# Retention attention and routed experts on one core: the passage from attention to the first expert is rearranged (digits of nine chunks at once, search tables in halves on VectorE, rows in half blocks, two weight chunks ahead of the gather)

## Chip, cores and metric

The kernel runs on one core of a Trainium2 chip. The metric is device time in microseconds (us) of one execution, taken as the median of several runs. Engines: PE is TensorE (matrix products), DVE is VectorE, ACT is ScalarE, POOL is GpSimd, SP is the engine that here issues the plain DMAs.

## What is computed

The reference, cut to what matters: a causal retention attention, and a mixture of experts with one expert per token, whose tokens are handed out greedily in the order of their logits and with a fixed capacity of 576 for each of the eight experts.

```python
# attention: B=8, H=8, S=576, D=64
scores = scale * np.matmul(q, k.transpose(0, 1, 3, 2))
ret = scores * Dmat[None]            # gamma[h] ** (i - j) for i >= j, else 0
x = np.matmul(ret, v)                # then laid out as 4608 tokens x 512
# experts: N=4608 tokens, D=512, E=8, F=1024, cap=576
logits = x @ w_gate
for idx in np.argsort(-logits.flatten()):
    tok, e = idx // E, idx % E
    if assigned[tok] >= 0 or counts[e] >= cap: continue
    assigned[tok] = e; counts[e] += 1
for e in range(E):
    mask = assigned == e
    out[mask] = np.maximum(x[mask] @ w1[e], 0.0) @ w2[e]
```

## The kernel before

**Attention** (lines 484 to 847) works through 16 units, four batch pairs of four head pairs each; a unit has nine blocks of 128 positions. For every batch pair it leaves the transposed tokens in the tile `xT` (four head pairs of 128 rows by 1152 tokens). Out of these come the logits (`logits`, `logits2`), in 36 chunks of 128 tokens, nine per batch pair, and the tokens as rows in a DRAM buffer `xd`: by VectorE (`rows`) for the first three pairs, by PE (`rows_pe`, one block of 128 tokens, four head pairs, a ScalarE copy L711 and a write to `xd` on SP's queue L712) for the last. The table `fill`, written through `at(g, ...)`, says after which block a piece of this side work stands in the program.

**Routing** is done expert by expert: the kernel finds which expert fills first, at which logit, and lists its tokens. The first such search (`search_first`, L250) looks for the bound digit by digit, in five digits of 7, 7, 6, 6 and 6 bits. It needs, for every chunk, the digits of the best logit (`first_digits`, tiles `DF` and `D2`) and a table of comparisons for each digit from the second on (`first_table`, tiles `FT`). In the kernel before, digits of the last nine chunks are made three chunks at a time, interleaved with the counting of the first digit (`count_first`, `count_first_pe`); of the 128-wide table of these chunks, eight are made one by one by GpSimd (`first_table_slow`), the rest by VectorE during the search (`s.pending`). A round of the search is: PE sums flags (L259), VectorE takes the digit `j` (L261), marks the chunks' candidates `oe` (L269), updates the running value `vl`, `vf` (L275, L277), PE counts with the tables (L291, and L292 for what was carried), VectorE compares (L295 to L302). Where PE would idle, `s.idle` puts in a piece of the remaining `rows_pe` blocks, or matmuls on a constant tile (`warm`).

After the search come `members` and `listing` (the index tile `idx` of the first expert, L463), then `leave` (L483), which takes the expert's tokens out of the logits.

**Experts.** For each expert the rows of its 576 tokens are gathered in five pieces by GpSimd's indirect DMA (`gather`, L946, tile `xg`; four pieces of 128 tokens, one of 64), turned over by PE (`transposes`, L962) and split by ScalarE and VectorE into a rounded part `xh` and a rest `xl` (L964, L965). The weights come in eight chunks of 512 KB per expert (`dma_pump`, L916, SP's queue, tile `raw`, four buffers; chunks 0 to 3 are w1, 4 to 7 are w2). `conv` splits a chunk: ScalarE writes the rounded part (`w1h`, `w2h`, L930) and the negated copy (`w1l`, L934), and a GpSimd DMA adds `raw` to it (L935); with `fast` VectorE subtracts instead (L932). `l1` does 16 blocks of 12 matmuls (`ph`, L991: four contraction slices by three products of the parts; blocks alternate between 256 and 320 tokens, for expert 0 blocks 0 and 1 have 256, 2 and 3 have 320), each followed by ScalarE and VectorE (`hb`, L995, L998); two blocks in f use one w1 chunk with two token halves, so blocks 0 to 3 need chunk 0, 4 to 7 chunk 1, 8 to 11 chunk 2. `l2` (L1030, `py`) does the second product.

What orders the work: engines run their own queues in program order. `Mixer` interleaves the routing of the next expert (`phases`) with the matmuls by estimated times. `state['most']` caps how many weight chunks `dma_pump` may issue, so it decides at which place of SP's queue a load stands. In the kernel before, four chunks are issued as soon as the first expert is known, one is converted (`fast`) before its tokens arrive, and three more after blocks 0, 1 and 2 of `l1`.

```python
state = dict(dma=0, conv=0, most=4, listing=-1)          # before, L876
        gather(0)                                         # L1068
        conv(True)
        mix.step()
        warm(20)
```

Of the kernel before, what the change touches and what calls it, by code (L numbers as in the profile page):

```python
# [82 lines left out]
class Route:  # L83
# [14 lines left out]
    def setup(s):  # L98
# [17 lines left out]
        s.DF, s.inc, s.sm, s.oz, s.D1 = T("DF", [5, 36], BF16), T("inc", [5], I32), T("sm", [2, 5], I32), T("oe", [43, 8], BF16), T("D1", [36], F32)  # L116
# [53 lines left out]
    def first_digits(s, c0, c1):  # L170
# [8 lines left out]
        if c1 > 24:  # L179
            V.tensor_copy(s.D1[:, c0:c1], d[:, 1])  # L180
# [6 lines left out]
    def first_table(s, i, g0, g1):  # L187
        n, k = g1 - g0, widths(FIRST)[i]
        if k == 64:
            n *= 4  # L190
            s.nc.vector.tensor_tensor(s.FT[i][:, 4*g0:4*g1].rearrange("p c (k w) -> p c k w", w=2),
                                      s.k64[:, None, :].rearrange("p o (k w) -> p o k w", w=2).to_broadcast([128, n, 32, 2]),
                                      s.D2[:, i-2, 4*g0:4*g1, None, :].to_broadcast([128, n, 32, 2]), op=ALU.is_le)
            return
# [55 lines left out]
    def search_first(s):  # L250
# [5 lines left out]
        yield 300, 30  # L256
        for i, K in enumerate(KK):
# [15 lines left out]
            oh = s.oe  # L273
            t = pool.tile([128, 36], F32, name="vl")
# [3 lines left out]
            if i == 0 and len(s.pending) > 3:  # L278
                s.pending.pop(0)()
# [7 lines left out]
            for n, (a, b) in enumerate(pieces):  # L287
                yield 200, 25*(b - a)
                for c in range(a, b, w):
                    st = s.FT[i+1][:, c:c+2].rearrange("p c k -> p (c k)") if w == 2 else s.FT[i+1][:, c//4, :, c % 4]  # L290
                    nc.tensor.matmul(cw, st, s.oz[:, c+w-1:c+w+7].rearrange("p c e -> p (c e)"), start=(c == 0), stop=False, skip_group_check=True)  # L291
            nc.tensor.matmul(cw[:, 64-8*w:72-8*w], sel.to_broadcast([128, 128]), cp, start=False, stop=True, skip_group_check=True)  # L292
# [4 lines left out]
            else:  # L297
# [4 lines left out]
                V.tensor_tensor(cp[:64], own[0], x, op=ALU.add)  # L302
            s.idle("row")
# [76 lines left out]
    def members(s, p):  # L380
# [24 lines left out]
        if not p:  # L405
            s.idle("rows")
            s.idle(2)
# [9 lines left out]
    def listing(s, p):  # L417
# [25 lines left out]
        if not p:  # L443
            s.idle("rows")
            s.idle(6)
# [63 lines left out]
def attention(tc, nc, P, qk, vk, cst_d, wg_d, rf, xd, Lg):  # L509
# [187 lines left out]
    def rows_pe(bp, blk, product=False, hps=range(HP)):  # L697
# [4 lines left out]
        for hp in hps:  # L702
            o, x = pt[:, hp*128:(hp+1)*128], XT[bp][:, hp, blk*128:(blk+1)*128]
            if product:
                nc.tensor.matmul(o, x, ident, start=True, stop=True)
            else:
                nc.tensor.transpose(o, x, ident)
# [31 lines left out]
    for bp in range(NP):  # L739
        g0 = (bp+1)*4*NB + 2  # L740
        for k, b0 in enumerate((0, 3, 6)):
# [11 lines left out]
            else:  # L753
# [3 lines left out]
                else:  # L757
                    at(G-1, lambda it: rest(both(it, R.first_digits(27, 30))), it)
# [3 lines left out]
    for bp in range(3):  # L762
        g0, it = (bp+1)*4*NB + 2, R.first_digits(9*bp, 9*bp+9)
        for i in range(10):
            at(g0+22+i//3, next, it, None)
        for n, (i, a, b) in enumerate(((1, 0, 1), (1, 1, 2), (2, 0, 2), (3, 0, 2), (4, 0, 2))):
            at(g0+24+2*n, R.first_table, i, 2*bp+a, 2*bp+b)
# [59 lines left out]
    left = [lambda b=b: rows_pe(bp, b, b > 0) for b in range(NB)]  # L827
# [8 lines left out]
    R.first_table_slow(1, 24, 28)  # L836
    b = R.first_digits(30, 33)
# [42 lines left out]
def moe(tc, nc, P, R, xd, w1_d, w2_d, out, mix):  # L880
# [5 lines left out]
    state = dict(dma=0, conv=0, most=4, listing=-1)  # L886
    RAW, W1, W2, XH, XL = {}, {}, {}, {}, {}
    scat = []
    spacer = P['c'].tile([1, 1], F32, name="spacer")
# [79 lines left out]
    def l1(e, tr):  # L969
# [5 lines left out]
        for i, (f, s) in enumerate(order):  # L975
# [25 lines left out]
            if s and f in (1, 2, 4, 6) or e == 0 and i < 3:  # L1001
# [62 lines left out]
    def run():  # L1064
# [4 lines left out]
        conv(True)  # L1069
        mix.step()  # L1070
        warm(20)
# [3 lines left out]
        warm(3)  # L1075
# [74 lines left out]
```

## Time and profile before

| | us |
|---|---|
| median of 3 runs | 664.94 (661.15 to 668.07) |
| the profiled execution's own time | 667.28 |
| its span, first to last instruction | 665.5 |
| PE busy in the span | 633.5 (95%) |
| DVE busy | 420.1 (63%) |
| ACT busy | 273.1 (41%) |
| POOL busy | 180.7 (27%) |

The profile is of one execution. Times in rows are us from the span's start. A row of a timeline is a start, a duration, the engine, the line in the kernel, the operation, the tiles (written <- read), and the number of instructions merged; in square brackets stands how long the engine idled before it and what ended that. A row of the chain of waits is a start, a duration, and what the work that ended last was doing or waiting for then. PEclk is the share of TensorE's full clock that was granted.

### The profile page before, as it was taken

What the parts mean: (1) busy time and instruction counts of PE and PEld (TensorE: products, weight loads), DVE (VectorE), ACT (ScalarE), POOL (GpSimd) and SP (SyncE); (2) the same over time, 40 slices, a digit from 0 to 9 for tenths busy, and PEclk for the clock granted to TensorE, in tenths of its full rate; (3) what the DMA queues carried; (4) which work ended last, traced back from release to release, by engine and by line L of the source; (5) the groups of instructions that cost most, each with busy time, mean ns of one, the idle gap of its engine ahead of it and who ended that gap; (6) DMA issues with size and microseconds to landing.
All of it is one profiled execution on the core that took longest, in us unless ns stands there. A gap on an engine that the chain in (4) does not pass through costs nothing.

```text
span 665.5 us, 14105 instructions
## 1 busy us (share of the span) xinstructions
PE 633.5 (95%) x5381; PEld 542.3 (81%) x5383; DVE 420.1 (63%) x1603; ACT 273.1 (41%) x488; POOL 180.7 (27%) x233
## 2 busy tenths in 40 slices
PE   8999999999879998999999999998999999999995
PEld 6887877886659876987897798788879989978984
DVE  3577878788856987887897799587775302311200
ACT  2333333333227343554356156334724733652601
POOL 2221222122122116125143141332224134131111
PEclk8999999999988999999999999999999999999998
DMA  9995999974367749879499659928884995894521
GB/s 335 402 366 158 302 313 293 282 245 102 133 225 157 161 143 224 220 204 244 140 217 232 193 144 211 247 86 186 203 224 112 202 271 152 181 257 133 96 63 39
DMA packets 51699, 134.71 MB, mean 202 GB/s; under 512 B 5808, under 2 KB 19760, under 8 KB 51632
## 3 DMA queue, kind: packets, MB, share of 16 engines
q1 hardware_dynamic: 36528, 81.65, 36.5%
q0 software_dynamic: 14960, 51.91, 35.7%
q8 instruction: 42, 0.69, 0.4%
q10 hardware_dynamic: 144, 0.26, 0.1%
q14 instruction: 25, 0.20, 0.1%
HBM read 81.90 MB, written 18.87 MB: 151 GB/s over the span
## 4 chain that ended last, share of the span: by engine, by line
PE 66%; DVE 13%; issue 10%; DMA 6%; ACT 2%; POOL 2%; SPq 0%; POOLq 0%; DVEq 0%; ACTq 0%
PE py L1030 24%; PE ph L991 20%; PE pA L584 4%; PE pX L636 4%; PE pX L626 3%; PE pS L601 3%; DMA qin<-in_qk 2%; PE pt L962 2%; DMA raw<-in_w 2%; PE r L341 2%; PE pT L665 1%; DVE G L168 1%; PE pX L624 1%; DMA cst<-in_cst 1%; DMA w2l<-raw 1%
## 5 line engine op out<-in xcount | busy, mean ns | idle before, releaser
L1030 PE MATMUL py<-w2h,hb 128*128 128x512 f32 x576 | 188.3, 399 | 0.0
L991 PE MATMUL ph<-xh,w1h 128*128 128x320 f32 (+1 forms) x512 | 153.7, 305 | 1.4 <-ACT xh L964 0.7
L991 PE MATMUL ph<-xl,w1h 128*128 128x320 f32 (+1 forms) x512 | 150.5, 298 | 1.0 <-issue 1.0
L991 PE MATMUL ph<-xh,w1l 128*128 128x320 f32 (+1 forms) x512 | 150.4, 298 | 0.0
L1030 PE MATMUL py<-w2l,hb 128*128 128x512 f32 (+1 forms) x320 | 125.5, 392 | 0.1
L1030 PEld LDWEIGHTS py<-w2h,hb 128*128 128x128 f32 x576 | 104.0, 188 | 20.7
L991 PEld LDWEIGHTS ph<-xh,w1h 128*128 128x128 f32 x512 | 97.6, 193 | 3.7 <-ACT xh L964 1.6
L991 PEld LDWEIGHTS ph<-xl,w1h 128*128 128x128 f32 x512 | 97.3, 192 | 1.8 <-issue 1.2
L998 DVE SCALAR_TENSOR_TENSOR hb<-ph,hb 128x256 fp32r<-128x256 f32 (+1 forms) x192 | 58.8, 351 | 61.9 <-ACT hb L995 57.0
L991 PEld LDWEIGHTS ph<-xh,w1l 128*128 128x128 f32 x512 | 97.4, 192 | 0.0
L995 ACT ACTIVATE hb<-ph 128x256 fp32r<-128x256 f32 (+1 forms) x128 | 51.4, 409 | 106.6 <-PE ph L991 98.5
L607 ACT ACTIVATE S<-pS,cst 64x128 f32<-64x128 f32 x128 | 46.4, 363 | 96.6 <-PE pS L601 94.9
L1007 POOL DMA_INDIRECT out_y<-yt,idx x40 | 40.9, 1022 | 118.2 <-ACT yt L1047 75.4
L1030 PEld LDWEIGHTS py<-w2l,hb 128*128 128x128 f32 (+1 forms) x320 | 56.7, 177 | 14.0 <-DMA w2l<-raw 1.5
L564 POOL TENSOR_TENSOR ks<-nin,cst 128x512 f32<-128x512 f32 x32 | 33.3, 1058 | 113.7 <-DMA nin<-in_vk 102.4
L1047 ACT ACTIVATE yt<-py 128x512 f32<-128x512 f32 x32 | 19.1, 598 | 105.3 <-PE py L1030 79.7
L935 POOL DMA_DIRECT2D w2l<-raw x32 | 28.9, 902 | 122.5 <-ACT hb L995 118.7
L589 DVE TENSOR_TENSOR am<-pA,cst 128x512 f32<-128x512 f32 x64 | 41.1, 683 | 22.1 <-PE pA L584 15.6
L946 POOL DMA_INDIRECT xg<-xd,idx x40 | 40.4, 1010 | 51.7 <-issue 27.0
L1050 DVE TENSOR_TENSOR yt<-yt,py 64x512 f32<-64x512 f32 x8 | 5.4, 679 | 69.9 <-ACT yt L1049 69.8
L935 POOL DMA_DIRECT2D w1l<-raw x31 | 27.7, 907 | 59.4 <-ACT w1l L934 36.8
L584 PE MATMUL pA<-qin,kin 64*128 64x128 f32 x512 | 38.3, 289 | 1.6 <-DMA qin<-in_qk 1.6
(190 smaller groups left out, 968.7 us busy)
## 6 DMA issues: line engine op xcount, KB each, us to landing
raw<-in_w SPq DMA_DIRECT2D x64, 512.0 KB, 6.5
w2l<-raw POOLq DMA_DIRECT2D x32, 512.0 KB
w1l<-raw POOLq DMA_DIRECT2D x31, 512.0 KB
kin<-in_qk SPq DMA_DIRECT2D x14, 576.0 KB
qin<-in_qk SPq DMA_DIRECT2D x14, 576.0 KB
vin<-in_vk SPq DMA_DIRECT2D x14, 576.0 KB, 11.0
nin<-in_vk SPq DMA_DIRECT2D x14, 512.0 KB, 7.7
xd<-xr SPq DMA_DIRECT2D x36, 192.0 KB, 4.2
```

The costliest lines, as they stand in the source:

```text
L564: nc.gpsimd.tensor_tensor(KS[u][:, a:b], LD[u, 'n'].rearrange("p (a d) -> p a d", d=64)[:, a:b], ks[:, u % HP, a:b, None].to_broadcast([12 ...
L584: nc.tensor.matmul(PA[0][h][:, j], LD[u, 'k'][r, s], LD[u, 'q'][r, s], start=True, stop=True, skip_group_check=True)
L589: nc.vector.tensor_tensor(am, PA[0][h], m[:, None, h, :].to_broadcast([128, n, 128]), op=ALU.mult)
L607: nc.scalar.activation(st[64*h:64*h+64, :, 64*h:64*h+64], PS[u][64*h:64*h+64], AF.Copy, scale=ss[64*h:64*h+64, hp, c:c+1])
L636: nc.tensor.matmul(px[64*h:64*h+64, :], v[:, blk*128+64*h:blk*128+64*h+64], AM[g, h], start=False, stop=blk < 8, skip_group_check=True)
L935: nc.gpsimd.dma_start(lo, raw, accum_op=ALU.add)
L946: nc.gpsimd.indirect_dma_start(out=xg[:n, j, :], out_offset=None, in_=xd[:, :], in_offset=bass.IndirectOffsetOnAxis(ap=found[e][:n, j:j+1] ...
L991: T.matmul(ps, w, x, start=(k == 0), stop=(k == 11))
L995: A.activation(hb[:, f, c], ps, AF.Relu)
L998: V.scalar_tensor_tensor(hb[:, f, to+a:to+b], ps[:, a:b], 0.0, hb[:, f, 256*s+a:256*s+b].bitcast(F32), op0=ALU.max, op1=ALU.subtract)
L1007: st = nc.gpsimd.indirect_dma_start(out=out[:, :], out_offset=bass.IndirectOffsetOnAxis(ap=found[e][:n, t:t+1], axis=0), in_=y[:n], in_off ...
L1030: T.matmul(ps[:m], a, w, start=(k == 0), stop=(k == last), skip_group_check=True)
```

## The change

- **Digits**: `first_digits` for chunks 27 to 35 is one call of nine chunks instead of three of three; its first two instructions stand ahead of the last count, and the copy `D1` is gone.
- **Tables**: `first_table_slow` is gone. VectorE makes the 128-wide table of the last twelve chunks in one instruction in the search's first round, and the three 64-wide tables in halves of six chunks. One table of the third batch pair stands earlier in attention.
- **Search**: the product for what was carried (L292) stands between the two pieces of the counting matmuls. Idle places of PE are filled otherwise: rows are plain transposes in half blocks, `"rows"` is one such half and two constant matmuls, and `members` and `listing` have constant matmuls only.
- **Weights**: two chunks are issued before the gather, both are converted fast. A 1-element DMA on SP's queue reads the third gathered piece, and the next loads stand behind it. The other six chunks of expert 0 are converted after blocks 3, 5, 7, 9, 11 and 13. There are 25 and 4 constant matmuls around the first transposes in place of 20 and 3.

```diff
@@ first_digits, first_table
-        if c1 > 24:
-            V.tensor_copy(s.D1[:, c0:c1], d[:, 1])
...
-    def first_table_slow(s, i, c0, c1):
-
-        for c in range(c0, c1):
-            k = widths(FIRST)[i]
-            s.nc.gpsimd.tensor_scalar(s.FT[i][:, c//4, :, c % 4], s.kt[:, :k, 0], s.D1[:, c:c+1], None, op0=ALU.is_le)
@@ search_first
         yield 300, 30
+        s.idle("row")
...
             oh = s.oe
+            if i == 0:
+                s.pending.pop(0)()
             t = pool.tile([128, 36], F32, name="vl")
...
-            if i == 0 and len(s.pending) > 3:
-                s.pending.pop(0)()
             if s.pending:
                 s.pending.pop(0)()
...
-            nc.tensor.matmul(cw[:, 64-8*w:72-8*w], sel.to_broadcast([128, 128]), cp, start=False, stop=True, skip_group_check=True)
+                if n == 0:
+                    nc.tensor.matmul(cw[:, 64-8*w:72-8*w], sel.to_broadcast([128, 128]), cp, start=False, stop=False, skip_group_check=True)
...
+            if s.pending:
+                s.pending.pop(0)()
             s.idle("row")
@@ attention, its end
-            at(g0+24+2*n, R.first_table, i, 2*bp+a, 2*bp+b)
+            at(g0+24-2*(bp == 2)+2*n, R.first_table, i, 2*bp+a, 2*bp+b)
...
-    some(3)
-    rest(both(R.count_first(33, 36), b))
-    R.first_table_slow(1, 28, 32)
-    c = R.first_digits(33, 36)
+    some(4)
+    rest(R.count_first(33, 36))
+    c = R.first_digits(27, 36)
+    for _ in range(2):
+        next(c)
     R.count_first_pe([27, 30, 33], **tag())
     rest(c)
-    R.pending = [lambda: R.first_table(1, 8, 9)] + [lambda i=i: R.first_table(i, 6, 9) for i in (2, 3, 4)]
-    some(1)
-    return R, [lambda b=b, h=h: rows_pe(bp, b, True, h) for b in range(NB - len(left), NB) for h in [(x,) for x in range(HP)]]
+    R.pending = [lambda: R.first_table(1, 6, 9)] + [lambda i=i, a=a, b=b: R.first_table(i, a, b) for i in (2, 3, 4) for a, b in ((6, 7.5), (7.5, 9))]
+    return R, [lambda b=b, h=h: rows_pe(bp, b, h) for b in range(NB - len(left), NB) for h in (range(2), range(2, HP))]
@@ moe
-    state = dict(dma=0, conv=0, most=4, listing=-1)
+    state = dict(dma=0, conv=0, most=2, listing=-1)
...
-            if s and f in (1, 2, 4, 6) or e == 0 and i < 3:
+            if e == 0 and i == 4:
+                state['most'] = 8*E
+            if i in ((3, 5, 9, 13) if e else (3, 5, 7, 9, 11, 13)):
                 conv()
...
         conv(True)
+        conv(True)
         mix.step()
-        warm(20)
+        warm(25)
...
-        warm(3)
+        warm(4)
...
-        state['most'] = 8*E
+
+        nc.sync.dma_start(spacer2, XG[0][0:1, 2, 0:1])
+        state['most'] = 4
+        dma_pump()
```

On VectorE, at the end of attention and the start of the search, there stand before the digits of the last three chunks alone (`om`, `dg`, `DF`, `D` are what `first_digits` writes, `f` and `cp` come of the first count, `j` is the first digit):

```order
L248 TENSOR_TENSOR cp_2297<-cnt,room_473 128x8
L156 TENSOR_SCALAR om<-m 128x3
L158 TENSOR_TENSOR om<-m,om 128x3
L177 TENSOR_TENSOR dg<-om,sm 128x5x3
L177 TENSOR_TENSOR dg<-dg,sm 128x5x3
L180 CAST D_490<-dg 128x3
L181 TENSOR_TENSOR DF<-dg,inc 128x5x3
L183 TENSOR_TENSOR D_491<-dg,inc 128x3x6
L261 TENSOR_REDUCE j<-r 128x1
```

and now those of all nine, whose two `om` have already run, and behind the marks `oe` the tables `FT`:

```order
L240 TENSOR_TENSOR cp_2282<-cnt,room_473 128x8
L177 TENSOR_TENSOR dg<-om,sm 128x5x9
L177 TENSOR_TENSOR dg<-dg,sm 128x5x9
L179 TENSOR_TENSOR DF<-dg,inc 128x5x9
L181 TENSOR_TENSOR D_490<-dg,inc 128x3x18
L254 TENSOR_REDUCE j<-r 128x1
L262 SCALAR_TENSOR_TENSOR oe<-DF,j,oh 128x112
L265 TENSOR_SCALAR sel<-rc_f,j 128x1
L262 SCALAR_TENSOR_TENSOR oe<-DF,j,oh 128x176
L193 TENSOR_TENSOR FT_497<-kt,DF 128x1536
L270 TENSOR_SCALAR vl<-DF,j 128x36
L272 TENSOR_TENSOR vf<-vl,DF 128x36
```

Three digit instructions fewer stand between `cp` and `j`, and a table of 1536 elements in place of 512 stands between `oe` and `vl`.

On SP's queue, where the first expert `e` is read, there stood before:

```order
L712 DMA xd<-xT 128x512 x8
L896 TENSOR_LOAD e
L896 ISA x2
L712 DMA xd<-xT 128x512
L916 ISA
L916 DMA raw<-in_w 128x1024
```

and now (`spacer` is the 1-element DMA):

```order
L703 DMA xd<-xT 128x512 x9
L885 TENSOR_LOAD e
L885 ISA x2
L905 ISA
L905 DMA raw<-in_w 128x1024
L905 ISA
L905 DMA raw<-in_w 128x1024
L1072 DMA spacer_2290<-xg 1x1
L905 ISA
L905 DMA raw<-in_w 128x1024
```

The last write to `xd` has moved ahead of the reading of `e`, and from the third weight chunk on every load stands behind the wait for gathered tokens.

On ScalarE, where the first expert's blocks begin, there stood before:

```order
L930 ACTIVATE w1h<-raw 128x1024
L964 ACTIVATE xh<-pt 128x4x128 x2
L995 ACTIVATE hb<-ph 128x256
L930 ACTIVATE w1h<-raw 128x1024
L934 ACTIVATE w1l<-raw 128x1024
L964 ACTIVATE xh<-pt 128x4x128 x2
L964 ACTIVATE xh<-pt 128x4x64
L995 ACTIVATE hb<-ph 128x256
```

and now:

```order
L919 ACTIVATE w1h<-raw 128x1024 x2
L953 ACTIVATE xh<-pt 128x4x128 x2
L984 ACTIVATE hb<-ph 128x256
L953 ACTIVATE xh<-pt 128x4x128 x2
L953 ACTIVATE xh<-pt 128x4x64
L984 ACTIVATE hb<-ph 128x256
L984 ACTIVATE hb<-ph 128x320 x2
L919 ACTIVATE w1h<-raw 128x1024
L923 ACTIVATE w1l<-raw 128x1024
```

The second chunk is rounded before the tokens come, and the third only after block 3 (`hb` of 320). Behind the first expert's transposes PE's and DVE's instructions stand in the same order as before; ACT's and POOL's differ only in where the conversions of expert 0 stand.

## Rows read from the trace of the kernel before

**Rows 1.** The page: busy time of PE, its share of the span, instructions.
```profile
PE 633.5 (95%) x5381; PEld 542.3 (81%) x5383; DVE 420.1 (63%) x1603; ACT 273.1 (41%) x488; POOL 180.7 (27%) x233
```
**Rows 2.** The chain that ended last: start, us, what.
```profile
181.67 0.36 SPq L916
...
201.44 4.65 DMA w1l<-raw
...
206.56 6.08 DMA raw<-in_w
...
290.08 5.97 DMA w2l<-raw
...
553.62 25.59 PE ph L991 x192
```
**Rows 3.** Windows of 1 us: each engine's busy time, then PEclk, DMA share, GB/s.
```profile
193.00:194.00 1.00, 0.00 (x0) 0.00 (x0) 0.93 (x4) 0.00 (x0) 0.40 (x1) 0.84 0.93 307
...
203.00:204.00 1.00, 1.00 (x5) 1.00 (x5) 0.86 (x5) 1.00 (x2) 0.00 (x0) 0.54 1.15 221
```
**Rows 4.** Timeline of DVE, 167 to 196 us.
```profile
167.49 0.17 DVE L247 TENSOR_TENSOR f<-cnt,room 128x8 bf16<-128x8 f32 x1
...
168.70 0.16 DVE L261 TENSOR_REDUCE j<-r 128x1 f32<-128x8 f32 x1
...
169.97 0.42 DVE L195 TENSOR_TENSOR FT<-kt,DF 128x512 bf16<-128x512 bf16 x1
...
172.79 0.55 DVE L191 TENSOR_TENSOR FT<-k,D 128x768 bf16<-128x768 bf16 x1
...
179.09 0.17 DVE L261 TENSOR_REDUCE j<-r 128x1 f32<-128x8 f32 x1 [0.28 <-PE r L259]
...
185.59 0.67 DVE L463 SCALAR_TENSOR_TENSOR idx<-lo 32x5 int32<-32x5 f32 x4
187.61 1.23 DVE L932 TENSOR_TENSOR w1l<-raw,w1h 128x1024 fp32r<-128x1024 f32 x1 [1.36 <-ACT w1h L930]
188.76 0.45 DVE L470 TENSOR_TENSOR t<-oh,ge 128x288 bf16<-128x288 bf16 x1
...
193.39 0.68 DVE L965 TENSOR_TENSOR xl<-pt,xh 128x512 fp32r<-128x512 f32 x1
```
**Rows 5.** Timeline of PE, 169 to 230 us.
```profile
169.28 1.48 PE L291 MATMUL r<-oe,FT 128*128 128x64 bf16 x36 [0.28 <-DVE oe L269]
...
185.04 4.49 PE L1107 MATMUL warm<-full 128*128 128x512 bf16 x19
...
190.88 0.53 PE L962 MATMUL pt<-ident,xg 128*128 128x128 f32 x4 [0.74 <-DMA xg<-xd,idx]
...
194.18 0.72 PE L962 MATMUL pt<-ident,xg 128*128 128x128 f32 x4 [2.10 <-DMA xg<-xd,idx]
...
195.59 1.22 PE L991 MATMUL ph<-xh,w1h 128*128 128x256 f32 x4
...
206.80 0.28 PE L991 MATMUL ph<-xh,w1h 128*128 128x256 f32 x1
...
218.40 0.39 PE L341 MATMUL r<-oh,G 128*128 128x32 bf16 x9 [1.64 <-DVE G L168]
...
229.91 0.71 PE L1030 MATMUL py<-w2h,hb 128*128 128x512 f32 x2
```
**Rows 6.** Timeline of POOL: the first expert's gather.
```profile
187.21 1.19 POOL L946 DMA_INDIRECT xg<-xd,idx  x1 [18.41 <-DMA raw<-in_w]
188.71 0.97 POOL L946 DMA_INDIRECT xg<-xd,idx  x1 [0.30 <-issue]
...
192.49 0.91 POOL L946 DMA_INDIRECT xg<-xd,idx  x1 [0.30 <-issue]
```
**Rows 7.** Timeline of ACT: conversions of weight chunks 0 and 1.
```profile
186.53 1.06 ACT L930 ACTIVATE w1h<-raw 128x1024 fp32r<-128x1024 f32 x1 [2.22 <-DMA raw<-in_w]
...
198.83 1.05 ACT L930 ACTIVATE w1h<-raw 128x1024 fp32r<-128x1024 f32 x1
```

More of the change, by code (lines that the diff above doesn't have):

```diff
@@ L189, in first_table @@
         if k == 64:
[L190 to L191 removed]
+            a, n = int(4*g0), int(4*n)
+            s.nc.vector.tensor_tensor(s.FT[i][:, a:a+n].rearrange("p c (k w) -> p c k w", w=2),
                                       s.k64[:, None, :].rearrange("p o (k w) -> p o k w", w=2).to_broadcast([128, n, 32, 2]),
[L193 removed]
+                                      s.D2[:, i-2, a:a+n, None, :].to_broadcast([128, n, 32, 2]), op=ALU.is_le)
             return
@@ L290, in search_first @@
                     st = s.FT[i+1][:, c:c+2].rearrange("p c k -> p (c k)") if w == 2 else s.FT[i+1][:, c//4, :, c % 4]
-                    nc.tensor.matmul(cw, st, s.oz[:, c+w-1:c+w+7].rearrange("p c e -> p (c e)"), start=(c == 0), stop=False, skip_group_check=True)
-            nc.tensor.matmul(cw[:, 64-8*w:72-8*w], sel.to_broadcast([128, 128]), cp, start=False, stop=True, skip_group_check=True)
+                    nc.tensor.matmul(cw, st, s.oz[:, c+w-1:c+w+7].rearrange("p c e -> p (c e)"), start=(c == 0), stop=(c + w == 36), skip_group_check=True)
+                if n == 0:
+                    nc.tensor.matmul(cw[:, 64-8*w:72-8*w], sel.to_broadcast([128, 128]), cp, start=False, stop=False, skip_group_check=True)
             if w == 1:
@@ L405, in members @@
         if not p:
-            s.idle("rows")
-            s.idle(2)
+            s.idle(6)
         yield (3000 if 0 < p < E - 1 else 1550 if not p else 1900), 125
@@ L443, in listing @@
         if not p:
-            s.idle("rows")
-            s.idle(6)
+            s.idle(9)
         for g0, g1 in ((0, 9),) if p else ((0, 5), (5, 9)):
@@ L695, in rows, with rows_pe @@
                                   TR[0][32*a:32*a+32].rearrange("p b h i -> p b (h i)"))
-    def rows_pe(bp, blk, product=False, hps=range(HP)):
+    def rows_pe(bp, blk, hps=range(HP)):
         if 0 in hps:
@@ L703, in rows_pe @@
             o, x = pt[:, hp*128:(hp+1)*128], XT[bp][:, hp, blk*128:(blk+1)*128]
[L704 to L707, printed above, removed]
+            nc.tensor.transpose(o, x, ident)
         if HP - 1 not in hps:
@@ L757, in attention @@
                 else:
-                    at(G-1, lambda it: rest(both(it, R.first_digits(27, 30))), it)
+                    at(G-1, rest, it)
         if bp < NP-1:
@@ L764, in attention @@
         for i in range(10):
-            at(g0+22+i//3, next, it, None)
+            at(g0+22-2*(bp == 2)+i//3, next, it, None)
         for n, (i, a, b) in enumerate(((1, 0, 1), (1, 1, 2), (2, 0, 2), (3, 0, 2), (4, 0, 2))):
-            at(g0+24+2*n, R.first_table, i, 2*bp+a, 2*bp+b)
+            at(g0+24-2*(bp == 2)+2*n, R.first_table, i, 2*bp+a, 2*bp+b)
     kscale(0)
@@ L826, in attention @@
     bp = NP-1
-    left = [lambda b=b: rows_pe(bp, b, b > 0) for b in range(NB)]
+    left = [lambda b=b: rows_pe(bp, b) for b in range(NB)]
     def some(n):
@@ L885, in moe @@
     regs, XG = {}, {}
-    state = dict(dma=0, conv=0, most=4, listing=-1)
+    state = dict(dma=0, conv=0, most=2, listing=-1)
     RAW, W1, W2, XH, XL = {}, {}, {}, {}, {}
     scat = []
-    spacer = P['c'].tile([1, 1], F32, name="spacer")
+    spacer, spacer2 = [P['c'].tile([1, 1], F32, name=f"spacer{i}") for i in range(2)]
     def phases():
@@ L1115, in idle @@
             def idle(what):
-                if what not in ("row", "rows"):
-                    warm(what)
-                    return
-                for _ in range(1 + (what == "rows")):
+                if what in ("row", "rows"):
                     if rows:
@@ L1124, in idle @@
                         warm(1)
+                    what = 2*(what == "rows")
+                if what:
+                    warm(what)
             R.idle = idle
```

4 lines of the change are left out of this document (1 added, 3 removed).

## The prediction

> **What bounds the kernel now.** I read the page first: PE is busy for 95% of the span [rows 1], so a change can gain only where PE waits, works slowly or fills in with constant matmuls. The page's slices show that between attention and experts, at about 165 to 220 us, and I read that stretch engine by engine. It falls into four parts.
>
> The first is a VectorE chain. Between the first count's flags at 167.49 and the first digit at 168.70 VectorE works through the last three chunks' digits [rows 4]. The search's five digits then take until 179.09, and the index tile is done at 185.59 + 0.67 = 186.26 [rows 4]. PE only serves here; its 36 counting matmuls take 1.48 [rows 5].
>
> The second is the arrival of the tokens. The gather starts at 187.21, 0.95 after the index, and its second piece at 188.71 [rows 6]. Piece 0 is issued by 188.40 and is there at 190.88, 2.5 later; piece 1 is issued by 189.68 and is there at 194.18, 4.5 later [rows 5, 6]. What lies beside it is the weights: four chunks, issued from 181.67 [rows 2], of which the first arrives at 186.53 [rows 7]; the DMA engines are 0.93 busy while piece 1 is awaited [rows 3].
>
> The third is the clock. [...]
>
> The fourth is the weights' recycling. Chunk 1's accumulating DMA lands 4.65 after 201.44, only then is a buffer free for the load that takes 6.08 from 206.56 [rows 2]; ScalarE stands before that chunk, VectorE behind ScalarE, and PE waits 1.64 for a table of the second search at 218.40 [rows 5].
>
> **The change, part by part.** I add up gains on the profiled execution, whose time is 667.28, 2.34 above the median of 664.94; the gain is then taken from the median.
>
> *Digits and tables.* Six digit instructions replace 21. Seven of the 21 stand between flags and digit, which are 1.21 apart [rows 4]; four are left, so about 0.3 goes. The other fourteen lie between counting instructions; by the same 0.17 each (1.21/7) they are worth 2.4 if none is hidden, and nothing if all lie in the counting's own latencies. I take 0.9, the lower half, since they were interleaved to fill those. One table moved ahead in attention stands before an `xT` that PE waits for: a loss of a 512-wide table, 0.42 [rows 4], at worst; I take 0.2. Sum: 1.0 earlier, bounds -0.1 and 2.7.
>
> *Search.* VectorE's 128-wide table grows from 512 to 1536 elements. From 512 in 0.42 to 768 in 0.55 [rows 4] is 0.51 ns an element, so it takes about 0.94. It starts after `oe`, near where the short one starts, and the last twelve counting matmuls need it: 0.5 more on VectorE, of which PE's first 24 matmuls (24/36 of 1.48) hide most. I charge 0.1. In rounds two and three half a table (0.2) leaves the way between `vf` and the comparison; its other half lies beside PE's next flag sum. Moving L292 inside shortens PE's end and delays its second piece alike: nothing. Cover gone, the halves come back as 0.2 a round. Sum: 0.2 earlier, bounds -0.5 and 0.5. The index is then done at 186.26 - 1.2 = 185.05.
>
> *Rows in half blocks.* The last write to `xd` goes out before the expert is read, so SP issues the first weights as soon as it has the register: about 180.0 against 181.67. By the old latency (186.53 - 181.67 = 4.9) chunk 0 is there by 184.9 and, with half the traffic, chunk 1 by 186. PE's constant matmuls fill idle places only; 25 of them at 4.49/19 last 5.9, from about 183.8 to 189.7, and are over when piece 0 comes.
>
> *Two fast conversions.* VectorE pays a second 1.15 (187.61 to 188.76, [rows 4]) before `leave`: 185.05 + 2.3 = 187.4. `leave` takes 4.63 (188.76 to 193.39), to 192.05; two `xl` of 0.65 end at 193.3; before, block 0 began at 195.59 [rows 5], with the second `xl`.
>
> *Gather.* It starts 0.95 after the index, at 186.0. Five pieces are issued over 6.2 (187.21 to 192.49 + 0.91, [rows 6]). With the two weight chunks landed by then, each piece needs the 2.5 of piece 0 (itself beside traffic; I let the range run from 1.5 to the 4.5 of piece 1): piece 1 is there at 190.95, piece 2 by 192.2, piece 4 at 194.7. The first gather instruction, beside the fast conversion, took 1.19 and the next 0.97 [rows 6], so the second conversion costs the gather 0.2 at most by the rows. [...]
>
> *First four blocks.* A block at full clock lasts 1.6 (25.59 for 192 matmuls, [rows 2]; 0.133 each). Block 0 runs its first eight matmuls at about 192, waits for `xl` to 193.3, ends at 193.8; the other three transposes, of which the last waits for piece 4, end at 195.1; blocks 1 to 3, one of 256 and two of 320 tokens, take 5.0. Block 4 starts at 200.1 against 206.80: 6.7 earlier, the index's 1.2 among it.
>
> *Loads behind the 1-element DMA.* SP waits for piece 2, to 192.2. Queued behind it are all further weights; chunk 2 is there 4.9 later, at 197.5, and ScalarE wants it after block 3, at 200.5: covered by 3. Its conversion starts its accumulation 2.6 later (198.83 to 201.44, [rows 2, 7]), and 4.65 on it lands: 207.75. Block 8 wants it 48 matmuls and two counting groups after 200.1, at 207.2: a new wait of 0.5. The old wait of 1.64 goes, since chunk 5's buffer is now free from 187.4 on and it is loaded right behind chunks 2 to 4; I leave 0.3 for VectorE's search behind a ScalarE that converts after every second block, and 0.3 for the last w2 chunk, converted late in both. So l2, which began at 229.91 [rows 5], runs 6.7 + 1.64 - 0.5 - 0.3 - 0.3 = 7.2 earlier. From there PE's and VectorE's orders are unchanged and each load hangs on them, so the gain stays: **664.94 - 7.2 = 657.7**.
>
> **Rivals.** *The clock falls all the same.* For it: the waits for `xl` and piece 4, and that it fell here before. Against: before, PE idled 0.74 and 2.10 with only constant matmuls between [rows 5]; in my schedule no gap reaches 1 us. Price: about 5.5 us of matmuls and transposes up to block 4 take twice as long, less the waits that they then cover (1.3): 4.2, so 661.9. [...]
>
> *The accumulations bound.* Six of them now start within some 17 us, and one in the row took 5.97 where the other took 4.65 [rows 2]. With 1.3 more each, block 8 waits 1.3 longer and w2's last chunks in l2 about as much again: 2.6, so 660.3. Against: the first of the six starts when no load is under way.
>
> *Slower: the clock falls already in the search.* Then the counting (1.48 [rows 5], and three rounds of half as many matmuls: 2.2), the listing (18 wider matmuls, taken as 1.5) and the first blocks all run at half clock: 5.2 more before the index and 5.5 after, 10.7 against 7.2 gained: 668.4. It decides if the clock falls before about 175; if it stays down longer, each block costs 1.6 more. Against: that stretch kept the full clock before, and now has more constant matmuls.
>
> *It doesn't do what it says*: if the fourteen hidden digits gain nothing and the long table is fully exposed, 1.4 is missing: 659.1. That is inside my forecast's range.
>
> **How the numbers follow.** Forecast 0.70, clock in l1 0.13, accumulations 0.12, slower 0.05. The forecast's own range is 654 to 660.5. Down: 1.7 more from digits and 0.3 from the search at their upper bounds, 0.6 if pieces take 1.5, 1.1 if none of the three new waits comes, 3.7 in all. Up: 1.1 and 0.7 at the lower bounds and 2 if pieces take 4.5, of which I take three quarters, as all three at once are unlikely. The range of 8 in 10 takes in the first two rivals: 653 to 663. One per cent, 6.65 us, is about what a measurement of this kernel can tell from no change; it lies at 658.3. A little under three quarters of the forecast's share is below that: 0.51 faster. The rest of it, the first two rivals and the milder part of the last are within 1%, 0.46; 0.03 of the last, with a clock that stays down, is slower.
>
> **What would show it.** Right: the first digit near 167.7 and the index near 185; the first weights issued near 180; pieces 2.5 after their issue; PEclk 1.00 through 190 to 205; block 4 at 200 and no wait at the third counting group. Wrong: a PEclk near 0.5 after 190, ScalarE waiting for chunk 2 after block 3, PE waiting long for w1's rest at block 8 or 12, or a later stage longer than before by what was gained here.

## The result, and the profile after

The changed kernel takes 657.72 us (median of 10 runs, 656.33 to 661.91), the kernel before beside it 665.04 (10 runs, 661.15 to 668.07). The ratio on record is 0.9912, with a 95% interval of 0.9892 to 0.9933: 0.7 to 1.1% faster. One slow run each of e1 (670.89), e8 (994.03) and e9 (669.45) is in the medians of the table below, and not in the ratios.

The profiled execution of the changed kernel lasts 656.7, its span 654.9. The page's first rows answer to [rows 1]; PE is still busy nearly all the time.

```profile
span 654.9 us, 14063 instructions
...
PE 627.4 (96%) x5371; PEld 535.2 (82%) x5371; DVE 421.2 (64%) x1591; ACT 272.3 (42%) x487; POOL 174.1 (27%) x224
```

VectorE's timeline of the changed kernel, to be held against [rows 4] (start, duration, line, operation, tiles; in brackets the idle time before it):

```profile
155.42 0.28 DVE L583 TENSOR_TENSOR am1t<-pA1t,cst 128x128 f32<-128x128 f32 x1
...
167.36 0.17 DVE L239 TENSOR_TENSOR f<-cnt,room 128x8 bf16<-128x8 f32 x1
...
168.23 0.16 DVE L254 TENSOR_REDUCE j<-r 128x1 f32<-128x8 f32 x1
...
169.12 0.95 DVE L193 TENSOR_TENSOR FT<-kt,DF 128x1536 bf16<-128x1536 bf16 x1
...
178.23 0.17 DVE L254 TENSOR_REDUCE j<-r 128x1 f32<-128x8 f32 x1 [0.27 <-PE r L252]
...
184.73 0.66 DVE L457 SCALAR_TENSOR_TENSOR idx<-lo 32x5 int32<-32x5 f32 x4
185.43 1.23 DVE L921 TENSOR_TENSOR w1l<-raw,w1h 128x1024 fp32r<-128x1024 f32 x1
187.52 1.22 DVE L921 TENSOR_TENSOR w1l<-raw,w1h 128x1024 fp32r<-128x1024 f32 x1 [0.86 <-ACT w1h L919]
188.66 0.45 DVE L464 TENSOR_TENSOR t<-oh,ge 128x288 bf16<-128x288 bf16 x1
...
193.30 1.28 DVE L954 TENSOR_TENSOR xl<-pt,xh 128x512 fp32r<-128x512 f32 x2
```

From flags to first digit are 0.87 instead of 1.21, from first to last digit 10.00 instead of 10.39; the table of 1536 takes 0.95. The first row shown is the last mask product of attention (line 583); in the kernel before the row is this one:

```profile
154.55 0.27 DVE L589 TENSOR_TENSOR am1t<-pA1t,cst 128x128 f32<-128x128 f32 x1
```

So attention came to that point 0.87 later here. I do not put that to the change: in the runs below the same row lies anywhere between 153.74 (e12) and 158.02 (e3), and e2, with the old attention, has it at 157.83. The mean granted clock goes with it in part: it is 0.990 to 0.993 in the six profiles that reach the row last (e1, e2, e3, e8, e10 and e11, 157.10 to 158.02), and 0.994 to 0.997 in the others but three, 0.987 in before and 0.991 in e4 and e6, which had it at 0.50 behind the row. From that row on I count: to the first digit 14.15 before, 12.81 after; to the index instruction 31.04 before, 29.31 after.

GpSimd's, SP's and ScalarE's timelines, beside [rows 6], the SPq row of [rows 2] and [rows 7]:

```profile
186.71 1.15 POOL L935 DMA_INDIRECT xg<-xd,idx  x1 [37.74 <-DVE w1l L921]
188.16 1.43 POOL L935 DMA_INDIRECT xg<-xd,idx  x1 [0.30 <-issue]
189.90 0.96 POOL L935 DMA_INDIRECT xg<-xd,idx  x1 [0.30 <-issue]
```

```profile
180.06 0.91 SPq L905 DMA_DIRECT2D raw<-in_w  x2
193.28 0.73 SPq L1072 DMA_DIRECT2D spacer<-xg  x1
194.24 2.46 SPq L905 DMA_DIRECT2D raw<-in_w  x4
```

```profile
186.43 1.06 ACT L919 ACTIVATE w1h<-raw 128x1024 fp32r<-128x1024 f32 x1 [1.03 <-DMA raw<-in_w]
```

PE's timeline, beside [rows 5]: the first two transposes wait a quarter of a microsecond each, block 0 starts at 193.16, block 4 at 201.43, l2 at 222.83.

```profile
190.31 0.53 PE L951 MATMUL pt<-ident,xg 128*128 128x128 f32 x4 [0.26 <-DMA xg<-xd,idx]
...
191.97 0.51 PE L951 MATMUL pt<-ident,xg 128*128 128x128 f32 x4 [0.24 <-DMA xg<-xd,idx]
...
193.16 0.74 PE L980 MATMUL ph<-xh,w1h 128*128 128x256 f32 x4 [0.24 <-ACT xh L953]
...
194.64 0.74 PE L980 MATMUL ph<-xl,w1h 128*128 128x256 f32 x4 [0.27 <-DVE xl L954]
...
201.43 0.28 PE L980 MATMUL ph<-xh,w1h 128*128 128x256 f32 x1
...
222.83 0.70 PE L1021 MATMUL py<-w2h,hb 128*128 128x512 f32 x2
```

The windows of the same stretch (PE busy, granted clock, DMA share, GB/s), beside [rows 3]: the granted clock, in the kernel before 0.50 from 194 to 203, is 1.00.

```profile
193.00:194.00 1.00, 0.84 (x7) 1.00 0.67 205
194.00:197.00 3.00, 2.73 (x25) 1.00 0.68 194
197.00:203.00 6.00, 6.00 (x53) 1.00 0.75 287
203.00:204.00 1.00, 1.00 (x9) 1.00 0.00 0
```

Between 202 and 232 the list of PE's waits is empty; the wait of 1.64 for the table G is gone and no other has come. L2 starts 7.08 earlier than at 229.91 [rows 5], and the y tiles of the first four experts keep a distance of 7.0 to 7.3. The two profiles end 10.6 apart, 3.5 more. Most of it lies in expert 4 (from the l2 of expert 3 to that of expert 4 it is 61.58 before and 58.77 after). PE's waits there, of the kernel before (440 to 475) and of the changed kernel (432 to 467), in us in total, times, longest:

```profile
PE r L341 <- DVE G L168: 2.6, 2, 1.5
PE ph L991 <- issue: 1.0, 1, 1.0
```

```profile
PE r L337 <- DVE G L168: 1.1, 1, 1.1
```

A wait of PE for nothing but its own instructions ("issue"), 1.0, makes VectorE's next table late by 1.5 in turn. All eight profiles of e5 to e12 have this stall (0.9 to 1.0), in texts of both sorts, the changed kernel's own among them (e11); e1 and e4 don't have it. So it belongs to neither kernel, and the 10.6 is not all the change's doing; e11's ratio of 0.9926, with the stall in its profile, is that of the first comparison.

### The profile page after: what moved, and what is told of

It is laid out like the page before. It is cut to its first block, busy times and chain, and to the rows that moved or that the text cites. A ratio compares the mean times of both kernels' runs of the same rounds, so it can differ in the third digit from the quotient of the medians.

```text
span 654.9 us, 14063 instructions
## 1 busy us (share of the span) xinstructions
PE 627.4 (96%) x5371; PEld 535.2 (82%) x5371; DVE 421.2 (64%) x1591; ACT 272.3 (42%) x487; POOL 174.1 (27%) x224
## 4 chain that ended last, share of the span: by engine, by line
PE 67%; DVE 13%; issue 9%; DMA 6%; POOL 2%; ACT 1%; SPq 0%; POOLq 0%; ACTq 0%; DVEq 0%
PE py L1021 24%; PE ph L980 22%; PE pA L578 4%; PE pX L630 3%; PE pX L620 3%; PE pS L595 3%; DMA qin<-in_qk 2%; PE pt L951 2%; PE r L337 1%; PE pT L659 1%; DMA raw<-in_w 1%; PE pX L618 1%; DMA cst<-in_cst 1%; DMA w2l<-raw 1%; DVE xr L683 1%
## 5 line engine op out<-in xcount | busy, mean ns | idle before, releaser
L1038 ACT ACTIVATE yt<-py 128x512 f32<-128x512 f32 x32 | 19.1, 598 | 104.6 <-PE py L1021 78.7
L935 POOL DMA_INDIRECT xg<-xd,idx x40 | 40.8, 1020 | 70.8 <-DVE w1l L921 37.7
```

Source lines behind the costliest of these rows:

```text
L935: nc.gpsimd.indirect_dma_start(out=xg[:n, j, :], out_offset=None, in_=xd[:, :], in_offset=bass.IndirectOffsetOnAxis(ap=found[e][:n, j:j+1] ...
```

## The experiments

The stretch from attention to l2 repeats better than whole runs, so I read each experiment by its rows too. Each kernel has one profile; where a kernel ran twice, A+B differs by 0.60 (changed and e11) and 0.41 (e7 and e12), so smaller differences say nothing. In the table, A is the time from the index instruction (line 457 or 463) to block 4, B from there to the first matmul of l2. The ratio is to the runs of the kernel before beside it.

| kernel | median us | ratio (95%) | A | B | A+B |
|---|---|---|---|---|---|
| before | 665.04 | | 21.21 | 23.11 | 44.32 |
| changed | 657.72 | 0.9912 (0.9892 to 0.9933) | 16.70 | 21.40 | 38.10 |
| e1 routing alone | 663.34 | 0.9972 (0.9955 to 0.9990) | 19.12 | 23.30 | 42.42 |
| e2 weights alone | 661.12 | 0.9950 (0.9927 to 0.9974) | 16.96 | 21.61 | 38.57 |
| e3 four chunks | 661.66 | 0.9974 (0.9954 to 0.9993) | 18.45 | 21.38 | 39.83 |
| e4 few constant matmuls | 658.54 | 0.9926 (0.9897 to 0.9955) | 18.62 | 21.39 | 40.01 |
| e5 subtractions after leave | 660.62 | 0.9891 (0.9863 to 0.9918) | 16.67 | 21.38 | 38.05 |
| e6 old places | 666.82 | 1.0006 (0.9983 to 1.0028) | 24.54 | 21.22 | 45.76 |
| e7 one fast conversion | 662.35 | 0.9919 (0.9890 to 0.9948) | 16.07 | 21.25 | 37.32 |
| e8 before, constant matmuls | 665.45 | 0.9974 (0.9945 to 1.0003) | 18.57 | 23.12 | 41.69 |
| e9 GpSimd busy later | 662.47 | 0.9928 (0.9903 to 0.9953) | 16.23 | 21.22 | 37.45 |
| e10 subtraction between | 662.07 | 0.9925 (0.9902 to 0.9948) | 16.82 | 21.23 | 38.05 |
| e11 changed again | 662.99 | 0.9926 (0.9898 to 0.9954) | 17.31 | 21.39 | 38.70 |
| e12 e7 again | 660.46 | 0.9903 (0.9883 to 0.9922) | 16.49 | 21.24 | 37.73 |

The kernel before had 664.38 beside e1 to e4, 666.48 beside e5 to e8, 666.61 beside e9 to e12.

**e1: the routing part alone.** The changed kernel with

```diff
-    state = dict(dma=0, conv=0, most=2, listing=-1)
+    state = dict(dma=0, conv=0, most=4, listing=-1)
-        conv(True)
         conv(True)
-        nc.sync.dma_start(spacer2, XG[0][0:1, 2, 0:1])
-            if i in ((3, 5, 9, 13) if e else (3, 5, 7, 9, 11, 13)):
+            if s and f in (1, 2, 4, 6) or e == 0 and i < 3:
```

> The changed kernel with the weights as before: four chunks ahead of the gather, one fast conversion, the old places of expert 0's conversions, no 1-element DMA. By the steps of the prediction (routing worth about 1, the rest worth about 6) the index is done 0.9 earlier than in the kernel before, the gather's second piece still comes 4.5 after its issue, PEclk still falls to half near 194 and block 4 starts near 205.9: about 664. Rival A, routing gives nothing by itself: 665. Rival B, the clock falls or stays with the routing part, because PE is kept busier there: PEclk 1.00 up to 205 and 660 or less.

Last mask product to index instruction: 29.30, as in the changed kernel, so 1.7 comes from this part and needs nothing of the other. The ratio is worth 1.9 (0.7 to 3.0), which speaks against both rivals. PE waits 3.01 for the first piece, and the granted clock falls, but only to about 197 (0.50 from 194 to 197, 0.90 from 197 to 198); in the kernel before, with the same weights, it stayed down until about 204 (0.50 from 194 to 203, 0.54 from 203 to 204).

**e2: the weights part alone**, the same lines put into the kernel before.

> The kernel before with the new weights alone: two chunks ahead of the gather, two fast conversions, the 1-element DMA, expert 0's conversions after every second block. By the steps: second piece 2.5 after its issue or less, PEclk 1.00 from 190 to 205, block 4 near 201.3 to 202.3, time 665.0 - 6.2 = 658.8. Rival A, the two parts need each other (the clock is kept only with the earlier index): PEclk half after 194, about 663. Rival B, the parts overlap, either alone gives nearly all: 657.7.

A+B is 38.57, 5.75 below before and 0.47 above the changed kernel; the granted clock is 1.00 from 180 to 212. The rows bear the theory out and speak against rival A. Against rival B: the parts add up, 0.28% and 0.50% alone by the ratios, 0.88% together. The whole time gained less than the theory's 6.2: the ratio is worth 3.3 (1.7 to 4.9). Part of the difference is that the profile of before lost more of the clock than most runs of that kernel (mean granted clock 0.987, the 24 runs beside e1 to e4 0.991 in median), which the rows count as gain; the rest stays open at n = 7.

**e3: four chunks ahead of the gather**, `most=4`, no 1-element DMA.

> The changed kernel with four chunks issued ahead of the gather as before, and so without the 1-element DMA; all else as changed. Theory (traffic delays the pieces, the wait lets the clock fall): second piece about 4.5 after its issue, PE idle for 1.5 or more before its transposes, PEclk half for some 10 us after it, block 4 near 205: 662 to 664. Rival A (traffic delays the pieces, but the clock stays, as more constant matmuls stand before them): block 4 near 203, 659 to 660. Rival B (the number of chunks is nothing; the fast conversion and the places did it): 657.5.

The pieces came late, as the theory had it, and the clock stayed, as rival A had it: the first was issued by 191.42 and was there at 195.60, and A is 18.45. That is 1.75 more than in the changed kernel's first profile and 1.14 more than in e11, its second, in which VectorE held the first gather instruction as it did here (2.20 there, 2.13 here). PE's first transposes, and the window of the idle time ahead of them:

```profile
195.60 0.54 PE L951 MATMUL pt<-ident,xg 128*128 128x128 f32 x4 [3.27 <-DMA xg<-xd,idx]
```

```profile
192.30:195.60 3.30, 0.03 (x3) 1.00 0.91 314
195.60:206.00 10.40, 10.16 (x77) 1.00 0.18 62
```

PE does nothing for 3.27, longer than the 2.10 of [rows 5], with the full clock granted throughout. The length of an idle stretch alone does not decide the fall. The whole times are nearer to the theory's 662 to 664 than these rows: the ratio is worth 1.7 (0.5 to 3.1). The profiled run had a mean granted clock of 0.993, the twelve runs 0.9905 in median, so most of the others lost clock that this profile kept; where they lost it is not shown.

**e4: 2 constant matmuls instead of 31**, `warm(25)` to `warm(2)`, the two others out.

> The changed kernel with 2 of its 31 constant matmuls between index and first block (25, 4 and 2 before). Theory: PE is idle for some 5 us before the first piece, PEclk falls to half there as it did in the kernel before, and blocks 0 to 3 run at half clock: 4.2 more, 661.9 (the price that the prediction gave this). Rival A: the clock doesn't depend on these, 657.5 or, as the transposes no longer queue behind them, 657. Rival B: the clock stays down longer than the first four blocks, 665 or more.

```profile
187.00:197.00 10.00, 4.92 (x26) 0.50 0.55 145
197.00:204.00 7.00, 7.00 (x55) 0.98 0.71 265
```

The clock falls near 187 and returns near 197, as long as in the kernel before. The price is 1.91 (40.01 against 38.10), or 1.31 against e11 (38.70), whose first gather instruction was held as it was here (2.09), and not 4.2: half of those ten microseconds PE waits for pieces anyway, and only the transposes and block 0 run slowly. The six runs have a mean granted clock of 0.986 in median, the changed kernel's ten 0.994: here the fall is not the profiled run's alone.

**e8: the kernel before with more constant matmuls**, `warm(20)` to `warm(26)` and `warm(3)` to `warm(13)`.

> The kernel before with 26 and 13 constant matmuls instead of 20 and 3 between the listing and the second transposes, so that PE has hardly a gap while the second piece is under way; nothing else changed. Theory (the clock's fall is some 2 to 3 of the gain): PEclk 1.00 through 190 to 206, index to block 4 about 21.3 instead of 24.10, in the median less, as not every run of the kernel before loses the clock as long: 662.5. Rival A, the clock falls all the same, as its cause isn't PE's gap: 24 and 664.4. Rival B, the constant matmuls hold up the transposes: 665 or more.

The windows of e8 and, after them, of the kernel before:

```profile
190.00:194.00 4.00, 3.95 (x19) 1.00 0.96 347
194.00:204.00 10.00, 8.75 (x62) 1.00 0.37 127
```

```profile
190.00:194.00 4.00, 1.34 (x8) 0.96 0.92 307
194.00:204.00 10.00, 9.82 (x47) 0.50 0.19 49
```

The clock is kept and A falls from 21.21 to 18.57: 2.64 is what the clock cost in the profiled execution of before. (The 24.10 and 21.3 of the expectation run to ScalarE's copy of block 4, 2.9 behind the start that A takes; by that count it is 21.46.) In whole times it is nearer 1.7, and may be nothing (ratio 0.9974, interval up to 1.0003).

**e6: expert 0's conversions early again**, behind blocks 0, 1, 3, 5, 9 and 13, all loads free behind the 1-element DMA.

> The changed kernel with expert 0's conversions at places like the old ones (two behind its first two blocks, four behind blocks 3, 5, 9 and 13), all loads free behind the 1-element DMA. Theory: ScalarE stands at chunk 2, which lands near 198, ahead of the xh of the last three pieces; block 2 starts near 201.5 instead of 197.9, some of it given back by earlier accumulations: 660 to 661. Rival A, the places are nothing: 657.7. Rival B, earlier accumulations are worth more than the wait: below 657.

The mechanism was right and its price more than twice as large. ScalarE stands 4.03 at chunk 2 with the xh of three pieces behind it, PE waits 4.94 for them, and then the granted clock falls as well (0.67 from 200 to 204, 0.50 from 204 to 208, 0.97 from 208 to 212):

```profile
200.18 1.06 ACT L919 ACTIVATE w1h<-raw 128x1024 fp32r<-128x1024 f32 x1 [4.03 <-DMA raw<-in_w]
```

```profile
203.48 1.43 PE L980 MATMUL ph<-xh,w1h 128*128 128x320 f32 x4 [4.94 <-ACT xh L953]
```

The whole gain is gone (A+B 45.76; ratio 1.0006), the 1.7 of the routing with it. With two chunks ahead of the gather the later places are no extra but a condition.

**e5: the two subtractions behind leave's first half and behind the second xl.**

> The changed kernel with VectorE's two w1l subtractions moved: the first behind the first half of the search's leave part, the second behind the second xl. Theory (GpSimd's gather instruction stands still while VectorE subtracts: beside a subtraction one took 2.0 to 2.1 in the runs so far, alone 0.95): the gather starts 0.95 after the index instead of 1.32, its second piece takes 0.95 instead of 1.43, block 0 starts about 0.8 earlier, index to block 4 is 18.3 instead of 19.13, time 656.9. Rival A (the late start has another cause, and the pieces wait for traffic): 19.1 and 657.7. Rival B (w1l now comes too late for block 0's second four matmuls): PE waits for VectorE's w1l before block 0 ends, 19.1 or more, 658 to 659.

Rival A's number came: to ScalarE's copy of block 4, to which the 18.3 and 19.1 run, it is 19.11, and A+B is 38.05 against 38.10. Of its reasons one held, that the late start has another cause: the gather started 1.32 after the index all the same. But it was not traffic that kept the pieces; the second gather instruction now met a subtraction:

```profile
187.13 1.15 POOL L937 DMA_INDIRECT xg<-xd,idx  x1 [36.77 <-DVE eb L481]
188.59 1.66 POOL L937 DMA_INDIRECT xg<-xd,idx  x1 [0.30 <-issue]
```

```profile
188.17 1.23 DVE L923 TENSOR_TENSOR w1l<-raw,w1h 128x1024 fp32r<-128x1024 f32 x1
```

The subtraction ends at 189.40, the gather instruction at 190.25, 0.85 later.

**e7: chunk 1 converted by ScalarE and an accumulating DMA**, the second `conv(True)` made `conv()`.

> The changed kernel with chunk 1 converted by ScalarE twice and an accumulating DMA, as the later chunks are, so that VectorE subtracts once. Theory: the second gather instruction takes 0.95 instead of 1.43 and leave ends 1.2 earlier, so the first block can end 0.5 earlier; chunk 1's accumulation is issued behind the gather near 193 and lands 4.6 to 6 later, 197.6 to 199, before block 4 wants it near 201: 657.2. Rival (its accumulation runs against the last pieces and chunks 2 and 3, and block 4 waits for it): 1 to 3 later, 659 to 660.5.

As the theory had it: second instruction 1.03, no wait for xl in block 0, A+B 37.32, 0.78 less. Block 4 doesn't wait for the accumulation. The whole time does not show it (ratio 0.9919).

**e9 to e12.** e9 is e7 with `nc.gpsimd.tensor_copy(seen, R.e[0:1, 0:1])` ahead of the gather; e10 is e9 with the subtraction behind `s.taken()`, leave's first three instructions; e11 is the changed kernel, e12 is e7.

> The kernel with one fast conversion, and one GpSimd copy of the first expert's number (1 element, some 5 before the index is done). Theory (the gather starts 1.32 after the index instead of the 0.95 of the kernel before because GpSimd has done nothing for 37 instead of 18): it starts 0.95 after the index; as that falls inside the first subtraction, it ends 1.03 after that one's end, 0.3 to 0.4 sooner than without the copy: index to l2 37.0 instead of 37.3. Rival (the 1.32 comes from the wait for VectorE's or ScalarE's work, or from elsewhere): start 1.32 after the index, 37.3.

> As the one with GpSimd's copy, and VectorE's one subtraction moved behind the first three instructions of leave, so that the first gather instruction starts just ahead of it and the second behind it. Theory (a gather instruction is held only if it starts while VectorE subtracts; one that started 0.3 or more before was not): first piece 1.15 to 1.2 long, second 0.95 to 1.1, pieces 0 and 1 some 0.4 earlier than with the copy alone, index to l2 36.6. Rival A (any overlap holds it): the first takes 2.0, 37.3. Rival B (the gather still starts 1.32 after the index, inside the subtraction): 37.8.

> The changed kernel again, beside the two above and on the same chip. From the first count's flags to the start of l2 it should repeat its 55.47 within 0.1, as nothing there hangs on chance but the clock; the difference to the earlier profile lies in attention (plus or minus 2) and in a wait for PE's instructions in expert 4 (0 or 2.9). Rival: the stretch itself varies by 1 or more, and the medians of the variants can't be told apart.

> The kernel with one fast conversion again, for its time beside the changed kernel's: index to l2 37.3 instead of 38.1, so 0.8 below the changed kernel in the medians, about 0.12 per cent, if the stretch is all that differs. Rival: the gain of the stretch is lost in later stages, medians equal or above.

e9's rival was right: still 1.33 after the index, with GpSimd idle for only 7.43 before it. In e10 the gather came inside the subtraction, as rival B had it, and was held:

```profile
189.38 2.06 POOL L937 DMA_INDIRECT xg<-xd,idx  x1 [7.43 <-DVE n L467]
```

In e11 A is 0.6 longer than in the first profile: my "within 0.1" was wrong. Chunk 1 was there sooner, so both subtractions ran without a gap (2.43 from 187.65) and the first gather instruction started inside the second:

```profile
188.91 2.20 POOL L935 DMA_INDIRECT xg<-xd,idx  x1 [36.77 <-DVE w1l L921]
```

e12 repeats e7's gain in the rows less well: 37.73 against e11's 38.70. Its median is 2.5 below e11's, but the intervals of the ratios overlap. One fast conversion was better in the stretch both times (0.8 and 1.0); that it is faster as a whole is not shown: with it the ratios are 0.9919, 0.9928 (e9) and 0.9903, with two 0.9912 and 0.9926.

## Why the prediction was right, and where its terms were not

The forecast was 657.7 and the median is 657.72. That closeness is luck. The ratio is worth 5.9 of 665.04 (4.5 to 7.2), so a gain of 7.2 is at the edge of what was measured. The gains were added up on a profile that had lost more of the clock than most runs of its kernel (0.987 against a median of 0.991 to 0.992 in the runs beside the experiments), and from the last mask product to l2 the profiles lie 7.95 apart and not 7.2. And terms erred against each other. The mechanisms were right in the main; these are the steps.

*Digits and tables: right.* Predicted 1.2 earlier (0.3 behind the flags and 0.9 ahead of them) and 0.2 lost. Measured: 0.34 from flags to digit and 1.00 from the last mask product to the flags, so the lower half of the 2.4 was the right choice. The moved table has no part in the 1.00: from the last mask product to the last `xT` it is 7.63 in both, and all the gain lies behind that. The table cost 0.1 further up: the last six mask products start within 6.43 in nearly all profiles with the new attention, and within 6.34 in before, e2 and e8. "The first digit near 167.7" came at 168.23 only because attention was late.

*Search: mis-sized, 0.39 instead of 0.2.* The first round grew by 0.22 (2.81 to 3.03), and each of the three after it shrank by 0.20 or 0.21. For rounds two and three that is the half table of the prediction. The fourth round has no table; there VectorE waited for the last PE matmul (line 292 of before), whose move I had costed at nothing. These are its rows, before and after:

```profile
178.38 0.17 DVE L300 COPY cn<-r 64x8 f32<-64x8 f32 x1 [0.39 <-PE r L292]
```

```profile
177.53 0.17 DVE L294 COPY cn<-r 64x8 f32<-64x8 f32 x1 [0.19 <-PE r L284]
```

*Weights' issue: right*, 180.06 against "about 180.0".

*Gather: too early by 0.85.* It started 1.32 after the index, not 0.95, and its second instruction took 1.43, not 0.95. I had read 0.2 at most from [rows 6]. There the first instruction started 0.4 ahead of the subtraction and the second 0.13 before its end, so the rows could not show a hold. The runs do: an instruction that starts while VectorE subtracts ends 0.84 to 0.86 after the subtraction's end (changed, e2, e5), or 1.02 to 1.03 if it is the first of the five (e3, e4, e6, e10, e11), and is up to 2.20 long. (e9's first, which came in the last 0.1 of a subtraction, took its usual 1.16.) It is not the subtraction alone. In nine profiles (e1, e3, e4, e6 to e9, e11, e12) gather instructions that start during another TENSOR_TENSOR of `leave`, 0.45 or 0.46 long, end 0.79 to 0.86 after it, first ones (e1, e7, e12) 1.02 or 1.03; the one exception, e5's first, started together with it. This is e7's first, which missed the subtraction:

```profile
187.67 1.33 POOL L935 DMA_INDIRECT xg<-xd,idx  x1 [37.75 <-DVE w1l L921]
```

```profile
187.52 0.45 DVE L464 TENSOR_TENSOR t<-oh,ge 128x288 bf16<-128x288 bf16 x1
```

A plain DMA of GpSimd was not held so in the one case that I compare: it started at 352.39 in the kernel before (L935), while a table of VectorE (L168, from 352.26, 0.76 long) had 0.63 still to run, took 0.89 (the median of its 31 in that profile is 0.87) and ended 0.26 after the table. What holds the gather instructions is not shown.

*First four blocks: 5.4 earlier, not 6.7.* Of the missing 1.3 the index, 0.86 earlier in these profiles instead of 1.2, is 0.34. The other 1.0 was lost on two paths side by side. One is the gather's 0.85. The other ended last: block 0's last four matmuls waited 0.27 more for `xl`. VectorE reached `xl` late because it waited 0.86 for ScalarE's rounding of chunk 1 (the row at 187.52), a term that the prediction put at nothing: it let the second subtraction follow the first at once, though a chunk that is there by 186 has 1.06 of rounding before it. In e11 VectorE had no such wait, and there the held gather alone made A 0.6 longer than here. Pieces took 2.4 from issue to transposes (189.59 to 191.97), near the 2.5 taken.

*Behind block 4: 1.7 gained, not 0.5.* The old wait went. The new wait at block 8, and the two charges of 0.3, did not come: PE waits for nothing from 202 to 232. (Chunk 2, by the prediction's own terms, comes at 192.2 + 4.9 = 197.1 and not 197.5; nothing hung on it.) These 1.1 made up for the 1.0 above.

*The clock rival's price: 4.2, measured 1.3 to 1.9* (e4). The mistake was to charge each matmul up to block 4 as slow, where PE was busy for only 4.92 of the ten microseconds at 0.50, and the clock was back before block 1 began (197.93). In the kernel before, too, the clock was back near 203.9 (0.54 from 203 to 204, 1.00 from 204 on), so all of block 3, from 205.04, and the end of block 2 ran with the full clock, and the price was 2.64.

So what are the 6.22 from index to l2? Going from before by e8 and e3 to the changed kernel: 2.63 is the clock (44.32 to 41.69), 1.86 the later places with the second fast conversion (to 39.83; 1.74 of it in B, where the wait for G was), and 1.73 two chunks fewer ahead of the gather (to 38.10). Against e11 instead of the first profile the last step is 1.13 and the sum 5.62; with one profile for most kernels each of these is good to about 0.6. e3 has the new routing and e8 the old, which A and B leave out as they start at the index. The routing adds 1.73, less the 0.1 in attention.

What stays open is the 0.37 by which the gather starts later. In the three profiles with 0.95 or 0.96 (before, e2, e8) VectorE stood idle for 1.2 or more behind the index; in all others it went on within 0.21 and the start came 1.32 to 1.33 after. The first three also have the old routing and all the others the new, and no run had the new routing and an idle VectorE. So what causes the later start is not shown.

## What to carry to other kernels

An operation that looks harmless beside another in one row may only have started first (the second gather instruction took 0.97 in [rows 6], and 1.43 and 2.01 in the changed kernel and e2): before two engines' work is laid side by side, look at which of the two was under way when the other began. When an engine is to work at once on what another one prepares, the preparing is a term of the sum. A half clock cost what the work in it cost, not what the time in it was (1.3 to 1.9 in e4, for ten microseconds at 0.50 with 4.92 of work), so take the waits out of the stretch before doubling it, and look where the clock comes back. A profile that lost more of the clock than its kernel's other runs (0.987 against 0.991) shows more to gain than they have. And when loads are held back to let a gather pass, move what consumes them too: e6 lost the whole gain by leaving the conversions in front of the gathered tokens.

## What the runs showed of the hardware

An idle PE kept the full granted clock (1.00) through 3.27 in e3, and lost it during 3.01 in e1 (0.95 from 192 to 194, 0.50 from 194 to 197), 2.10 in the kernel before (0.84 from 193 to 194, 0.50 from 194) and 4.94 in e6 (0.67 from 200 to 204, 0.50 from 204); it came back after some 3 in e1, 7 in e6 and 10 in before and e4. What decides if it falls, and when it comes back, is not shown. GpSimd's gather instructions, 0.91 to 0.96 in the changed kernel where no subtraction held them (1.15 to 1.19 the first of five in before, changed, e2, e5, e8 and e9), ended 0.79 to 1.03 after the end of a subtraction of VectorE, or of another TENSOR_TENSOR of `leave`, that had started before them, and took up to 2.20 (e6, e11); e9's first, which came in the last 0.1 of a subtraction, ended 1.06 after it. One plain DMA of GpSimd took 0.89 beside a table of VectorE and ended 0.26 after it. And a stall of 0.9 to 1.0 for PE's own instructions in expert 4 came and went with the runs and not with the kernel (e11 has it, the first profile of the changed kernel does not): with what follows it is worth about 2.8, as from the l2 of expert 3 to that of expert 4 it is 61.58 in the kernel before, with it, and 58.77 in the changed kernel, without it.
